# Reordering the value and gate products of a pair, and giving each step of the first block its own value tile

## Chip, cores, metric

One core of one Trainium2 chip. The metric is the device time of one execution in microseconds (us), as the median of several runs. PE is the matmul engine, DVE the vector engine, ACT the scalar engine, POOL the GpSimd engine, SP the engine that issues most DMAs.

## The reference, cut to what matters

```python
def reference(x, moe_w_gate, moe_w_val, moe_w_out):      # shortened
    X = np.fft.fft(x, axis=1)                            # x is 8 x 3008 x 256
    X = np.fft.fft(X, axis=2)
    y = X.real.reshape(24064, 256)
    gate = np.maximum(y @ w_gate, 0.0)                   # 256 x 1536
    val = y @ w_val
    return (gate * val) @ w_out                          # 1536 x 256
```

## The kernel before

The kernel folds the last transform into the two weights, and uses a symmetry of the real part: a column of the transform and its mirror image share an even part and differ in the sign of an odd part. So for one block of 512 columns and one slice of 128 features (a **step** `t`) it makes

- the gate: even product plus odd product gives the direct gate; a third product (`wm`, minus twice the odd weights) added to the same PSUM tile gives the mirrored gate;
- the value: even product `wc` into a PSUM tile `V`, then odd product `ws` on top. Between the two, DVE saves the even part: `E = nb * af + V`. Afterwards the mirrored value is `2E - V`.

There are 8 images x 3 blocks x 12 steps = 288 steps. From step 12 on they run as 144 - 6 = 138 **pairs** (pair `p` holds steps `2p` and `2p+1`), each with 16 projection matmuls (`out_piece`, line "po") of the block before. The first block (steps 0 to 11) has a simpler loop, without `E`, in which a third value product makes the mirrored value in place. The transform of the next image (`stage1`, `rotate`, `stage2`) is inserted at fixed steps by `between`, and POOL's folding of the images after that is dealt out by `pace`.

```python
psg = ...tile_pool(name="psg", bufs=2, space=PS)     # gate tiles
psv = ...tile_pool(name="psv", bufs=2, space=PS)     # value tiles, two banks each
...
ep = ...tile_pool(name="ep", bufs=3, space=SB)       # E and gm
...
def split(t):
    return t >= NF                                   # NF = 12

def pair(t, name):
    e = pairs.setdefault(t // 2, {})
    if name not in e:
        pool, shape, dt = {...,
                           "V": (psv, [128, 2, 512], F32), "gm": (ep, [128, 2, 512], F32),
                           "E": (ep, [128, 2, 512], F32)}[name]
        e[name] = pool.tile(shape, dt, tag=name.lower(), name=name)
    return e[name]

def gate(t):
    ...
    nc.tensor.matmul(G[:, ds], lhsT=wc[0][:, fs], rhs=pq[:, 0, ds], start=True, stop=False)
    nc.tensor.matmul(G[:, ds], lhsT=ws[0][:, fs], rhs=pq[:, 1, ds], start=False, stop=True)
    nc.scalar.activation(pair(t, "gs")[:, t % 2, ds], G[:, ds], ACTF.Relu)

def mirror_gate(t):                                  # must wait for the ReLU above
    ...
    nc.tensor.matmul(G[:, cols], lhsT=wm[0][...], rhs=pqt[b, blk][:, 1, cols], start=False, ...)
    nc.scalar.activation(pair(t, "gm")[:, t % 2, cols], G[:, cols], ACTF.Relu)

# value(t, k): the product with wc, ws or wm (k = 0, 1, 2) into pair(t, "V")[:, t % 2, :]
# even(t): E = nb * af + V           direct_h: h = gs * V         mirror_h: h = gm * (mirrored V)
# mirror_value(p): E = 2E - V on DVE for the whole pair, then mirror_h on POOL
...
def pace(t):
    paced["due"] += 0 if t < 22 else 1 if t < 46 else 0.85 if t < 100 else 0.7
    while paced["due"] >= 1:
        paced["due"] -= 1
        next(folds, None)
...
for t in range(NF + 1):                              # the first block
    if t:
        mirror_gate(t - 1)
    if t < NF:
        gate(t)
    if t:
        value(t - 1, 2)
        mirror_h(t - 1, 1, nc.vector, pair(t - 1, "V"))
    if t < NF:
        value(t, 0)
        value(t, 1)
        direct_h(t, 1)
        between(t)

for p in range(NF // 2, n + NF // 2):                # the pairs
    t = 2 * p
    live = p < n
    if NF // 2 < p <= n:
        mirror_gate(t - 1)
    if live:
        gate(t)
        value(t, 0)
    out_piece(t - NF, 0)                             # four projection matmuls
    between(t)
    if live:
        value(t + 1, 0)
    if NF // 2 < p <= n:
        direct_h(t - 2, 2)
    if live:
        even(t)
        even(t + 1)
    out_piece(t - NF, 1)
    if live:
        mirror_gate(t)
        gate(t + 1)
    out_piece(t + 1 - NF, 0)
    between(t + 1)
    if NF // 2 < p <= n:
        mirror_value(p - 1)
    if live:
        value(t, 1)
        value(t + 1, 1)
    out_piece(t + 1 - NF, 1)
```

## Time and profile before

| | before |
|---|---|
| median of 3 runs | 666.39 us (665.86 to 666.46) |
| profiled execution | 667.4 us |
| one steady pair without an insertion | 4.03 us (496 columns) to 4.11 us (512) |
| its matmuls back to back (512 columns: 10 x 0.216 + 16 x 0.109) | 3.90 us |
| first block, start of the first direct h to start of the last mirrored h | 32.1 us |

The head of the page: busy time of each engine, its share of the span, and its instructions.

```profile
PE 631.6 (95%) x4200; PEld 411.5 (62%) x4231; DVE 549.7 (82%) x642; ACT 433.2 (65%) x846; POOL 521.5 (78%) x436
```

PE at 95% looks full. The Trainium skill ("Perfetto Trace Analysis", Identifying the Most-Contended Engine) warns that matmul busy time is not a good measure of how close a kernel is to its limit, because matmuls are pipelined. This trace shows it: a 512-column matmul is listed with 0.38 us, but the next one starts 0.216 us later (and a 256-column one is followed after 0.109 us; medians over the trace). So PE must be judged by the **starts** of matmuls. Here is one pair of the last image, from the timeline (start, duration, engine, line and operation, output<-input, count; in brackets the idle time before, and what ended it). Only PE and DVE rows are kept.

```profile
605.80 0.38 PE L527 MATMUL V<-pq,wc 128*128 128x512 bf16 x1
606.02 0.60 PE L576 MATMUL po<-wo,h 128*128 128x256 bf16 x4
606.29 1.41 DVE L534 SCALAR_TENSOR_TENSOR E<-nb,af,V 128x512 f32<-128x512 bf16 x2 [0.48 <-PE V L527]
...
607.10 0.60 PE L576 MATMUL po<-wo,h 128*128 128x256 bf16 x4
607.61 1.21 DVE L554 SCALAR_TENSOR_TENSOR E<-E,V 128x1024 f32<-128x1024 f32 x1
607.75 0.59 PE L527 MATMUL V<-pq,ws 128*128 128x512 bf16 x2
```

The second even product starts at 605.80 and ends at 606.18. DVE has been idle for 0.48 us and starts the two `E` operations at 606.29; they end at 607.70. The odd product, which overwrites what `E` reads, starts at 607.75. PE's four projection matmuls before it, 0.109 us apart, end their slots at 607.54. The hole is 0.21 us, though the row of the odd product carries no bracket: in the modelled ends PE is still busy.

The first block has a hole of another kind. The lines are from step 5 of the first block:

```profile
52.70 0.67 DVE L547 TENSOR_TENSOR h<-gm,V 128x496 bf16<-128x496 f32 x1 [1.23 <-ACT gm L521]
53.43 0.37 PE L527 MATMUL V<-pq,wc 128*128 128x496 bf16 x1 [1.75 <-DVE h L547]
53.64 0.37 PE L527 MATMUL V<-pq,ws 128*128 128x496 bf16 x1
...
54.11 0.67 DVE L540 TENSOR_TENSOR h<-gs,V 128x496 bf16<-128x496 f32 x1 [0.74 <-PE V L527]
```

The even product of step 5 waits until DVE has finished the mirrored h of step 4, although the two use different halves of the `V` tile. DVE then waits 0.74 us for the product. The list of waits adds these up (total us, times, longest):

```profile
POOL h L547 <- DVE E L554: 107.7, 70, 4.1
DVE E L534 <- PE V L527: 61.5, 108, 2.6
PE V L527 <- DVE h L547: 7.7, 6, 1.7
PE psr L213 <- DMA t<-Td: 2.6, 1, 2.6
```

POOL's wait is spread unevenly. The windows view (length of the stretch, then busy us of each engine, with clock, DMA share and GB/s) shows that POOL is at 97 to 98% in one long stretch:

```profile
110.00:160.00 50.00, 48.41 (x342) 32.87 (x342) 42.03 (x48) 34.81 (x70) 49.06 (x46) 1.00 0.44 114
160.00:210.00 50.00, 49.70 (x350) 33.31 (x351) 43.34 (x49) 35.55 (x70) 48.58 (x43) 1.00 0.55 139
210.00:260.00 50.00, 49.49 (x337) 33.21 (x340) 43.46 (x49) 35.09 (x71) 49.07 (x44) 1.00 0.43 114
```

The fifth busy figure is POOL's: 49.06, 48.58 and 49.07 of 50 us.

Last, one stall at 400 us, where PE waits for the shuffled image, and after which the matmuls run at half speed (0.41 us apart) for a while:

```profile
399.74 0.60 PE L576 MATMUL po<-wo,h 128*128 128x256 bf16 x4
402.89 0.18 PE L213 MATMUL psr<-t,rot 128*128 128x12 bf16 x1 [2.56 <-DMA t<-Td]
...
403.97 0.62 PE L519 MATMUL G<-pq,wm 128*128 128x496 bf16 x1
404.38 0.62 PE L512 MATMUL G<-pq,wc 128*128 128x497 bf16 x1
```

### The profile page before, as it was taken

Reading aid. Unit: us, or ns where it says so; the run is one execution under the profiler, and the core shown is the slowest. Engines: PE = TensorE matmul, PEld = TensorE weight load, DVE = VectorE, ACT = ScalarE, POOL = GpSimd, SP = SyncE. Lnnn points to the kernel's source line nnn. Section 1 sums busy time; section 2 is a strip of 40 time slices with the busy share of each in tenths; the row PEclk is TensorE's granted clock in tenths of the full one; section 3 lists DMA queues with packets and bytes.
Section 4 is the critical chain, followed back from the end, with each engine's and each line's share of the span. In section 5 each row is a group of like instructions: output and inputs, shape, how many; then the busy total and the mean of one; then the engine's idle time right before and its main releaser. Section 6 shows DMA issues by size and latency. Waiting matters only on the chain.

```text
span 667.4 us, 11836 instructions
## 1 busy us (share of the span) xinstructions
PE 631.6 (95%) x4200; PEld 411.5 (62%) x4231; DVE 549.7 (82%) x642; ACT 433.2 (65%) x846; POOL 521.5 (78%) x436
## 2 busy tenths in 40 slices
PE   6867999999999999999999998999999999999995
PEld 3422576666666666666666665666666666666665
DVE  9845888888888888888888886888888888888881
ACT  5454586777677767676677765677677767656660
POOL 9559679999999999999988996988555555555552
PEclk9699999999999999999999998999999999999998
DMA  9593554542836184353724464211522142112114
GB/s 255 185 234 46 133 138 128 148 112 83 212 81 145 42 237 102 89 127 96 189 57 100 93 174 101 65 32 38 149 49 64 38 119 72 54 32 63 31 32 93
DMA packets 35635, 70.72 MB, mean 106 GB/s; under 512 B 6124, under 2 KB 23508, under 8 KB 32244
## 3 DMA queue, kind: packets, MB, share of 16 engines
q1 hardware_dynamic: 32152, 57.92, 33.2%
q0 software_dynamic: 3120, 11.80, 8.0%
q8 instruction: 33, 0.54, 0.3%
q10 hardware_dynamic: 304, 0.25, 0.2%
q14 instruction: 26, 0.21, 0.1%
HBM read 39.77 MB, written 30.96 MB: 106 GB/s over the span
## 4 chain that ended last, share of the span: by engine, by line
PE 78%; DVE 9%; POOL 5%; DMA 3%; issue 2%; ACT 2%; SPq 0%; DVEq 0%; POOLq 0%; ACTq 0%
PE po L576 32%; PE V L527 19%; PE G L513 8%; PE G L519 7%; PE G L512 7%; DVE E L534 6%; DMA t<-Td 2%; PE ps L183 2%; POOL eo L139 2%; PE ps L225 1%; POOL h L547 1%; PE psw L282 1%; DVE h L540 1%; DVE h L547 1%; DMA nb<-Nd 1%
## 5 line engine op out<-in xcount | busy, mean ns | idle before, releaser
L547 POOL TENSOR_TENSOR h<-gm,E 128x992 bf16<-128x992 f32 (+1 forms) x138 | 319.5, 2316 | 109.8 <-DVE E L554 107.7
L576 PE MATMUL po<-wo,h 128*128 128x256 bf16 (+2 forms) x2304 | 342.4, 273 | 0.7
L576 PEld LDWEIGHTS <-h 128*128 128x128 bf16 (+2 forms) x2304 | 233.2, 103 | 121.0 <-issue 0.5
L534 DVE SCALAR_TENSOR_TENSOR E<-nb,af,V 128x496 f32<-128x496 bf16 (+1 forms) x276 | 190.9, 733 | 79.2 <-PE V L527 61.5
L521 ACT ACTIVATE gm<-G 128x496 f32<-128x496 f32 (+1 forms) x288 | 170.2, 591 | 132.0 <-PE G L519 127.4
L540 DVE TENSOR_TENSOR h<-gs,V 128x1024 bf16<-128x1024 f32 (+3 forms) x150 | 172.7, 1151 | 8.6 <-PE V L527 7.5
L514 ACT ACTIVATE gs<-G 128x497 f32<-128x497 f32 (+2 forms) x288 | 169.6, 589 | 1.8 <-PE G L513 1.8
L554 DVE SCALAR_TENSOR_TENSOR E<-E,V 128x992 f32<-128x992 f32 (+1 forms) x138 | 164.3, 1190 | 0.0
L527 PE MATMUL V<-pq,wc 128*128 128x497 bf16 (+2 forms) x287 | 107.8, 376 | 7.7 <-DVE h L547 7.7
L513 PE MATMUL G<-pq,ws 128*128 128x497 bf16 (+2 forms) x287 | 107.8, 376 | 1.5 <-DVE pq L232 0.6
L519 PE MATMUL G<-pq,wm 128*128 128x496 bf16 (+1 forms) x288 | 108.2, 376 | 0.0
L512 PE MATMUL G<-pq,wc 128*128 128x496 bf16 (+2 forms) x271 | 101.7, 375 | 0.0
L527 PE MATMUL V<-pq,ws 128*128 128x496 bf16 (+2 forms) x276 | 82.6, 373 | 4.7 <-DVE E L534 2.2
L589 ACT COPY os<-po 128x512 f32<-128x512 f32 x63 | 36.9, 585 | 32.6 <-PE po L576 30.7
L513 PEld LDWEIGHTS <-ws 128*128 128x128 bf16 x288 | 28.2, 98 | 32.7 <-issue 0.3
L527 PEld LDWEIGHTS <-ws 128*128 128x128 bf16 x288 | 26.6, 97 | 32.6 <-issue 30.4
L193 ACT CAST t<-ps 96x512 bf16<-96x512 f32 x63 | 36.6, 581 | 12.3 <-PE ps L181 7.2
L527 PEld LDWEIGHTS <-wc 128*128 128x128 bf16 x288 | 28.2, 98 | 20.9 <-issue 3.2
L110 POOL TENSOR_TENSOR eo<-xla 94x254 bf16<-94x254 f32 x56 | 40.0, 724 | 1.0
L107 POOL TENSOR_TENSOR xla<-xla,xha 94x510 f32<-94x510 f32 x28 | 35.4, 1264 | 2.2
L110 POOL TENSOR_TENSOR eo<-xlb 94x254 bf16<-94x254 f32 (+1 forms) x42 | 33.6, 809 | 0.7
L519 PEld LDWEIGHTS <-wm 128*128 128x128 bf16 x288 | 28.2, 98 | 6.9 <-issue 4.1
(125 smaller groups left out, 381.8 us busy)
## 6 DMA issues: line engine op xcount, KB each, us to landing
out_dram<-os SPq DMA_DIRECT2D x126, 128.0 KB
out_dram<-os SPq DMA_DIRECT2D x86, 64.0 KB
Td<-t SPq DMA_DIRECT2D x7, 768.0 KB
t<-Td SPq DMA_DIRECT2D x7, 768.0 KB
xla<-in_x_dram SPq DMA_DIRECT2D x7, 720.0 KB
xlb<-in_x_dram SPq DMA_DIRECT2D x7, 640.0 KB
nb<-Nd SPq DMA_DIRECT2D x24, 128.0 KB
out_dram<-os SPq DMA_DIRECT2D x39, 48.0 KB
```

The source lines that it names most:

```text
L110: yield eng.tensor_tensor(e1[:, :, o:o + H - 1], x1[:, :, 1:H], free(x1, D - 1, [D, n], [-1, H - 1]), op=op)
L512: nc.tensor.matmul(G[:, ds], lhsT=wc[0][:, fs], rhs=pq[:, 0, ds], start=True, stop=False)
L513: nc.tensor.matmul(G[:, ds], lhsT=ws[0][:, fs], rhs=pq[:, 1, ds], start=False, stop=True)
L514: nc.scalar.activation(pair(t, "gs")[:, t % 2, ds], G[:, ds], ACTF.Relu)
L519: nc.tensor.matmul(G[:, cols], lhsT=wm[0][:, f * 128:(f + 1) * 128], rhs=pqt[b, blk][:, 1, cols], start=False, stop=True, skip_group_check ...
L521: nc.scalar.activation(pair(t, "gm")[:, t % 2, cols], G[:, cols], ACTF.Relu)
L527: nc.tensor.matmul(pair(t, "V")[:, t % 2, cs], lhsT=w[:, f * 128:(f + 1) * 128], rhs=pqt[b, blk][:, min(k, 1), cs], start=(k == 0), stop=( ...
L534: nc.vector.scalar_tensor_tensor(pair(t, "E")[:, t % 2, cols], nbt[b, blk][:, cols], af[:, f:f + 1], pair(t, "V")[:, t % 2, cols], op0=ALU ...
L540: nc.vector.tensor_tensor(pair(t, "h")[:, k, 0, 0:ds.stop - ds.start], pair(t, "gs")[:, k, ds], pair(t, "V")[:, k, ds], op=ALU.mult)
L547: eng.tensor_tensor(free(pair(t, "h")[:], 1024 * (t % 2) + 512 + w - 1, [1024, n], [-1, w]), pair(t, "gm")[:, k, cols], val[:, k, cols], o ...
L554: nc.vector.scalar_tensor_tensor(E[:, :, cols], E[:, :, cols], 2.0, V[:, :, cols], op0=ALU.mult, op1=ALU.subtract)
L576: nc.tensor.matmul(po[0:m, i, :], lhsT=pair(t - f + ff, "h")[:, ff % 2, sg, g * 128:g * 128 + m], rhs=wo[:, ff, :], start=(ff == 0), stop= ...
```

## The change

The intent: let DVE have both even products early, so that `E` is done before PE wants to add the odd products; and let the steps of the first block not wait for each other's `V` tile. No operation is added or removed.

```diff
     def pair(t, name):
 
         e = pairs.setdefault(t // 2, {})
+        if name == "V" and not split(t):
+            name = f"V{t % 2}"
+            if name not in e:
+                e[name] = psv.tile([128, 2, 512], F32, tag="v", name="V")
+            return e[name]
         if name not in e:
@@
             mirror_gate(t - 1)
         if live:
+            value(t, 0)
+            value(t + 1, 0)
             gate(t)
-            value(t, 0)
         out_piece(t - NF, 0)
         between(t)
-        if live:
-            value(t + 1, 0)
         if NF // 2 < p <= n:
             direct_h(t - 2, 2)
```

Below the inserted lines, line numbers of the changed kernel are 5 higher: L527 becomes L532, L534 L539, L554 L559, and so on.

## The prediction

> **What bounds the kernel now.** The page gives PE 95% busy, DVE 82%, POOL 78%, ACT 65% of 667.4 us. Busy PE overstates, so I read starts in the timeline. One 512-column matmul follows another by 0.213–0.216 us (the Trainium skill, "TensorE: Matmul & The Clock Gate", Part 1, has 215.7 ns; the trace agrees), a 256-column one by 0.108. A steady pair has 10 and 16 of these: 3.87 us. But pairs without inserted FFT work take 4.11 (E starts 606.29, 610.40, 614.52). The rest is a hole of 0.2 us ahead of the odd value product: PE stops at 607.53, V<-pq,ws starts at 607.75, right after the two E operations (606.29 + 1.41 = 607.70). These start 0.11 us after the second even product ended (605.80 + 0.38), DVE having idled 0.45 us. So the loop is second even product -> E, E -> odd product. I count 82 such holes, 16.5 us. Where stage1/stage2 is inserted in a pair's second half there is none.
>
> In the first block (38–71 us) the matmul starts show 15.7 us of gaps. The list of waits has V <- DVE h (L547) 7.7 us, 6 times, up to 1.75: every odd step's first value product waits for the mirrored h of the step before, which reads the other half of the same tile. DVE then idles 0.74 us before the direct h.
>
> **What the change does.** No work is added or removed.
>
> 1. First block: a tile per step removes the six waits. The gain per odd step is DVE's 0.74 us idle, not the wait; more where fold_w queued behind the blocked product (1.5 us at 53 us). Sum 5.5, less 0.8 because nb's DMA (5 us from pq to E at 118–123 us) then arrives just in time: **-4.7 us**.
> 2. Steady pairs: the second even product issues 0.43 us earlier, E about 0.4 earlier, ending before PE reaches the odd product. The hole closes: 0.197 each, 60 pairs outside stretch 4: **-11.8 us**.
> 3. Gate products issue 0.43 later; mirror_gate(t) follows only 8 matmuls after. gs starts 0.47 after the second gate product starts, takes 0.60, plus 0.05 to release PE: 1.12 against 1.08. New stall 0.035, some 78 pairs: **+2.7 us**.
> 4. POOL is 98% busy from 110 to 260 us (windows), mirrored h lagging E by 2–4 us with three E buffers. There POOL sets the pace; of 4.4 us of holes only about 1 is got: **-1 us**.
> 5. rotate waits for t<-Td at 400–403 us (2.6 us, then 3.4 us of half clock). DMA time doesn't shrink: **+0.6 us**.
>
> Sum -14.2: **652.3 us**, range 646.5 to 658.5, close to the 2% line (653.1): faster by over 2% 0.56, within 2% 0.43, slower by over 2% 0.01.
>
> **What would show each step.** (1) V<-pq,wc no longer waits for h L547; the first block ends 4–5 us earlier. (2) E pairs 3.9 us apart in the last block; no hole ahead of V<-pq,ws; E's wait for PE V (61.5 us) at most half. (3) G<-pq,wm in mid-pair starts 0.05 us after gs ends, with a PE gap of 0.02–0.06. (4) 110–260 us shrinks by 1–2 us only, POOL 99% busy, E or gm waiting more for POOL h. (5) psr's wait stays or grows.
>
> **What would make it wrong.** If os or t copies on ACT delay gs, the stall of (3) is 0.1 or more and eats half of (2). If POOL isn't the pace-maker, up to 3 us more. If rotate's wait and clock drop vanish, 4 us more; if more batches get one, 4 us less each. If ACT holds the first block, its gain halves.

## The result, and the profile after

| | before | after |
|---|---|---|
| median, same rounds, 4 runs each | 666.42 us | 648.12 us (646.91 to 649.26) |
| ratio | | 0.972 (95%: 0.9693 to 0.9747) |
| profiled execution | 667.4 us | 645.1 us |

Ratios are the mean time of one kernel's fast runs over that of the other's of the same rounds, so not quite the ratio of the medians. The change is faster by 18.3 us in the medians. The two profiles differ by 22.3 us: the profiled execution of before was a slow one of its kind (669.18 us as timed, against a highest of 668.38 among the timed runs), and the one of after the fastest of its four.

```profile
PE 618.7 (96%) x4231; PEld 410.4 (64%) x4231; DVE 549.3 (85%) x642; ACT 444.7 (69%) x846; POOL 521.9 (81%) x436
```

The steady pair, last image again:

```profile
584.66 0.59 PE L532 MATMUL V<-pq,wc 128*128 128x512 bf16 x2
...
585.31 0.38 PE L518 MATMUL G<-pq,ws 128*128 128x512 bf16 x1
585.41 1.40 DVE L539 SCALAR_TENSOR_TENSOR E<-nb,af,V 128x512 f32<-128x512 bf16 x2
585.52 1.04 PE L581 MATMUL po<-wo,h 128*128 128x256 bf16 x8
585.72 0.60 ACT L519 ACTIVATE gs<-G 128x512 f32<-128x512 f32 x1 [0.27 <-PE G L518]
586.40 0.38 PE L524 MATMUL G<-pq,wm 128*128 128x512 bf16 x1
...
587.04 0.60 PE L581 MATMUL po<-wo,h 128*128 128x256 bf16 x4
587.48 0.59 PE L532 MATMUL V<-pq,ws 128*128 128x512 bf16 x2
```

`E` now starts without waiting for PE and ends at 586.81; the odd product follows its predecessors at their own pitch (587.04 + 4 x 0.109 = 587.48, as listed). The hole is gone, and the five pairs of this image that took 4.11 us each now take 3.88 to 3.93. Counted by matmul starts over the whole traces from 72 us on, holes of more than 0.02 us ahead of the odd products fall from 79 (15.9 us) to 19 (4.8 us, 3.8 of them in four holes between 118 and 260 us). The mirrored gate product at 586.40 starts 0.08 us after `gs` ends (586.32), and 0.88 us after the first of eight projection matmuls, whose slots take 8 x 0.109 = 0.87: it comes just in time, and it does so everywhere: none of the mirrored gate products after 72 us has such a hole ahead of it.

Step 5 of the first block:

```profile
49.16 0.37 PE L532 MATMUL V<-pq,wc 128*128 128x496 bf16 x1
49.37 0.37 PE L532 MATMUL V<-pq,ws 128*128 128x496 bf16 x1
...
50.35 0.67 DVE L552 TENSOR_TENSOR h<-gm,V 128x496 bf16<-128x496 f32 x1 [1.23 <-ACT gm L526]
...
50.94 0.66 DVE L545 TENSOR_TENSOR h<-gs,V 128x496 bf16<-128x496 f32 x1
```

The products of step 5 run before the mirrored h of step 4, and DVE does the two h one after the other. The waits:

```profile
POOL h L552 <- DVE E L559: 51.7, 41, 2.1
DVE h L545 <- PE V L532: 40.5, 84, 1.9
DVE E L539 <- POOL h L552: 5.6, 10, 1.4
PE psr L213 <- DMA t<-Td: 1.4, 1, 1.4
```

"PE V <- DVE h of the mirror" is gone, and so is `E`'s wait for the even product (61.5 us before). DVE's slack hasn't vanished; it now lies before the direct h (40.5 us), where PE hardly waits for it (PE's own waits for the direct h come to 0.8 us). `E` waits longer for POOL (5.6 us, against 2.1 before). And POOL is as full as before in its stretch, which by the table below got no shorter:

```profile
110.00:160.00 50.00, 48.02 (x345) 32.95 (x343) 41.89 (x47) 36.69 (x71) 48.56 (x45) 1.00 0.45 117
160.00:210.00 50.00, 49.50 (x353) 33.38 (x352) 43.53 (x49) 36.17 (x70) 48.90 (x45) 1.00 0.57 144
210.00:260.00 50.00, 48.95 (x341) 32.75 (x341) 43.13 (x48) 36.14 (x69) 48.95 (x45) 1.00 0.49 134
```

A new stall lies in it, at the first block of the second image, where `E` needs the row `nb` that goes through DRAM:

```profile
116.09 0.39 PE L225 MATMUL ps<-m,t 128*128 128x128 bf16 x4
...
116.85 1.37 DVE L539 SCALAR_TENSOR_TENSOR E<-nb,af,V 128x496 f32<-128x496 bf16 x2 [2.71 <-DMA nb<-Nd]
...
118.28 0.58 PE L532 MATMUL V<-pq,ws 128*128 128x496 bf16 x2 [1.80 <-DVE E L539]
```

The rotation stall is shorter, and the clock stayed full after it:

```profile
390.35 0.18 PE L213 MATMUL psr<-t,rot 128*128 128x12 bf16 x1 [1.45 <-DMA t<-Td]
...
391.23 0.37 PE L524 MATMUL G<-pq,wm 128*128 128x496 bf16 x1
```

With the starts of `2E - V` (L554, L559), and of the first direct and the last mirrored h, as milestones, the 22.3 us of the two profiles split like this:

| stretch | before | after | difference |
|---|---|---|---|
| start to first direct h (unchanged code) | 39.0 | 38.5 | -0.5 |
| first block, to its last mirrored h | 32.1 | 26.0 | -6.1 |
| from there to pair 13 | 36.2 | 34.8 | -1.4 |
| pair 13 to 51 (POOL at 98%) | 159.7 | 159.9 | +0.2 |
| pair 51 to 83 | 133.2 | 128.8 | -4.4 |
| pair 83 to 85 (rotation stall) | 12.8 | 9.6 | -3.2 |
| pair 85 to 142 | 235.3 | 227.9 | -7.4 |
| to the end | 19.1 | 19.7 | +0.5 |

A warning about the milestone: in a steady pair `2E - V` starts 0.13 us before the odd product in the old order and 0.74 us before it in the new one. So some 0.6 us of the row up to pair 13 is no gain, and it comes back in the last row. At pair 51 `E` is late and the distance is 0.14 us in both, so by the odd product pairs 13 to 51 are 0.45 us shorter, not 0.2 longer, and pairs 51 to 83 gain about 3.8, not 4.4.

### The profile page after: what moved, and what is told of

It reads as the page before. It is cut to its first block, busy times and chain, and to the rows that moved or that the text cites. A ratio compares the mean times of both kernels' runs of the same rounds, so it can differ in the third digit from the quotient of the medians.

```text
span 645.1 us, 11866 instructions
## 1 busy us (share of the span) xinstructions
PE 618.7 (96%) x4231; PEld 410.4 (64%) x4231; DVE 549.3 (85%) x642; ACT 444.7 (69%) x846; POOL 521.9 (81%) x436
## 4 chain that ended last, share of the span: by engine, by line
PE 82%; DMA 5%; POOL 5%; DVE 3%; ACT 2%; issue 1%; SPq 1%; ACTq 0%; POOLq 0%; DVEq 0%
PE po L581 35%; PE V L532 17%; PE G L524 8%; PE G L518 8%; PE G L517 8%; DMA t<-Td 2%; DMA Td<-t 2%; PE ps L183 2%; POOL eo L139 2%; PE ps L225 1%; PE psw L282 1%; DVE E L539 1%; POOL h L552 1%; SPq L632 1%; DVE h L545 1%
## 5 line engine op out<-in xcount | busy, mean ns | idle before, releaser
L581 PE MATMUL po<-wo,h 128*128 128x256 bf16 (+2 forms) x2304 | 326.0, 272 | 0.0
L545 DVE TENSOR_TENSOR h<-gs,V 128x1024 bf16<-128x1024 f32 (+3 forms) x150 | 173.7, 1158 | 54.9 <-PE V L532 40.5
L539 DVE SCALAR_TENSOR_TENSOR E<-nb,af,V 128x496 f32<-128x496 bf16 (+1 forms) x276 | 190.2, 730 | 12.3 <-POOL h L552 5.6
L559 DVE SCALAR_TENSOR_TENSOR E<-E,V 128x992 f32<-128x992 f32 (+1 forms) x138 | 164.3, 1190 | 0.0
L517 PE MATMUL G<-pq,wc 128*128 128x497 bf16 (+2 forms) x288 | 107.9, 375 | 0.0
L532 PE MATMUL V<-pq,ws 128*128 128x497 bf16 (+2 forms) x288 | 85.4, 374 | 3.5 <-DVE E L539 3.4
L532 PE MATMUL V<-pq,wc 128*128 128x497 bf16 (+2 forms) x288 | 85.5, 375 | 0.0
L532 PEld LDWEIGHTS <-wc 128*128 128x128 bf16 x288 | 27.7, 98 | 22.5 <-issue 3.9
L517 PEld LDWEIGHTS <-wc 128*128 128x128 bf16 x288 | 28.2, 98 | 20.3 <-issue 2.9
L532 PEld LDWEIGHTS <-ws 128*128 128x128 bf16 x288 | 26.5, 97 | 9.7 <-issue 6.3
```

The costliest lines, as they stand in the source:

```text
L532: nc.tensor.matmul(pair(t, "V")[:, t % 2, cs], lhsT=w[:, f * 128:(f + 1) * 128], rhs=pqt[b, blk][:, min(k, 1), cs], start=(k == 0), stop=( ...
L539: nc.vector.scalar_tensor_tensor(pair(t, "E")[:, t % 2, cols], nbt[b, blk][:, cols], af[:, f:f + 1], pair(t, "V")[:, t % 2, cols], op0=ALU ...
L545: nc.vector.tensor_tensor(pair(t, "h")[:, k, 0, 0:ds.stop - ds.start], pair(t, "gs")[:, k, ds], pair(t, "V")[:, k, ds], op=ALU.mult)
L559: nc.vector.scalar_tensor_tensor(E[:, :, cols], E[:, :, cols], 2.0, V[:, :, cols], op0=ALU.mult, op1=ALU.subtract)
L581: nc.tensor.matmul(po[0:m, i, :], lhsT=pair(t - f + ff, "h")[:, ff % 2, sg, g * 128:g * 128 + m], rhs=wo[:, ff, :], start=(ff == 0), stop= ...
```

## The experiments

The theory after the result: (a) the first block's tiles and the pair's order are two independent gains that add; (b) in the pair, only the early second even product matters, the gate's place is free as long as `gs` ends in time; (c) from about 100 to 260 us POOL sets the pace and takes the gain there. Rivals are named with each run. "Same rounds" medians of before were 666.6 to 666.9 us.

### 1 and 2. Each part alone

Experiment 1 keeps only the hunk in `pair`, experiment 2 only the hunk in the loop over pairs.

```diff
# experiment 1, against before
+        if name == "V" and not split(t):
+            name = f"V{t % 2}"
+            ...
# experiment 2, against before
+            value(t, 0)
+            value(t + 1, 0)
             gate(t)
-            value(t, 0)
         ...
-        if live:
-            value(t + 1, 0)
```

Experiment 1, expected:

> Only the first block's value tile of its own per step; the old order of a pair. Theory (the two parts touch different stretches and add): the first block (first direct h to last mirrored h) shrinks from 32.1 to about 26.0 us as in the changed kernel, and the rest is as before: 660 us, 6 to 7 below the 666.4 of before; V<-pq,wc no longer waits for the mirrored h. Rival (what the first block gains is lost again, because POOL or the loads of nb set the pace later): 664 to 666 us. Rival (the tiles do little without the order): within 2 us of before.

Measured: 660.70 us, ratio 0.9904 (0.9881 to 0.9927), 5.9 below before. The first block took 26.03 us.

Experiment 2, expected:

> Only the new order of a pair; the first block keeps the shared tile. Theory: the first block stays at 32 us with its six waits; holes ahead of the odd value product are gone from the steady pairs, period 3.85 to 3.93 us in the last block; 655 us, 11 to 13 below before. Rival (the gain of the changed kernel is almost all the first block and the clock drop at 400 us that one profile of before happened to show): 661 us or more.

Measured: 654.13 us, ratio 0.9799 (0.9777 to 0.9821), 12.5 below before. The first block took 32.09 us, with its six waits (7.7 us).

What follows: 5.9 + 12.5 = 18.4 us, and the whole change gave 18.3. The parts add, and all of the gain is accounted for by the timed runs, so the 3 us of the rotation stall and the half clock in the two profiles need be no part of it: experiment 2 has its own drop of the clock (at 125 us, in its profile) and is as fast as the sum asks for. The granted clocks point the same way. In the rounds of these experiments before took 668.3 and 668.4 us in the two executions at a mean clock of 0.984, and 666.0 to 667.8 us in the five at 0.986 to 0.988; the profiled execution, at 0.984, is one of the former kind. Of the changed kernel's four, the two at 0.981 and 0.983 took 649.3 and 648.5 us, those at 0.986 and 0.987 took 647.8 and 646.9.

### 3. The gate products first again

```diff
         if live:
+            gate(t)
             value(t, 0)
             value(t + 1, 0)
-            gate(t)
         out_piece(t - NF, 0)
```

> The changed kernel with the gate products put back ahead of the two even value products, the latter still together and ahead of the projection. Theory (what counts is that the second even product comes before the first four projection matmuls; the gate's place costs and gives nothing, as gs ends just in time): the same as the changed kernel within 1.5 us, 647 to 649 us, with E starting about 0.4 us later in the cycle but still ending before the odd product. Rival, the term of the prediction (mirror_gate is held 0.035 us by gs in some 78 pairs): 2 to 3 us faster than the changed kernel, 645.5 us. Rival (E must start as early as it can): slower by 3 us or more, holes back.

Measured: 648.84 us (647.43 to 649.92), ratio 0.9716 (0.969 to 0.9743), against 0.972 for the change. The same, within noise. In its profile DVE waits 0.28 us for the second even product again (at 588.5 us), but `E` ends at 590.20 and the odd product starts at 590.48, at its own pitch. So the useful part of the reordering is that the second even product passes the four projection matmuls; that the gate goes behind both buys nothing and costs nothing. The prediction's stall of 2.7 us in the mirrored gate product isn't there: no execution of experiment 3, which keeps the gate out of its reach, was below 647.4 us.

### 4. POOL's load spread evenly

```diff
-        paced["due"] += 0 if t < 22 else 1 if t < 46 else 0.85 if t < 100 else 0.7
+        paced["due"] += 0 if t < 22 else 0.72
```

> The changed kernel with POOL's folds spread evenly (0.72 of a fold piece per step from step 22 on, in place of 1, then 0.85, then 0.7); the same work in all. Theory (POOL sets the pace from about 100 to 260 us: it is 98% busy there and E waits for it, so the new order gains nothing there): pairs 13 to 51 get shorter, the POOL lag stays under 1.5 us, the holes ahead of the odd product between 160 and 260 us (about 2 us) go, 3 to 4 us faster in all, 644.5 us; what is left is the wait for nb near 118 us. Rival (POOL is busy there but not the limit; stage1 and stage2 fill these pairs): within 1 us of the changed kernel.

Measured: 641.35 us (640.87 to 642.42), ratio 0.9614 (0.9591 to 0.9638), about 7 us below the changed kernel's 648.1: more than expected. (The two profiles differ by 5.5 us only; the changed kernel's is its fastest execution, and two of its four had a lower granted clock, as said above.) Pairs 13 to 51 took 154.8 us in place of 159.9, and pairs 18 to 51 (after the `nb` stall) 133.9 in place of 137.6. POOL's mirrored h followed `2E - V` by 0.6 us on average over pairs 13 to 51, in place of 2.8. In the windows POOL has slack again, and PE is listed as busy throughout:

```profile
160.00:210.00 50.00, 50.00 (x360) 34.32 (x359) 44.71 (x52) 37.10 (x71) 46.62 (x40) 1.00 0.46 123
210.00:260.00 50.00, 50.00 (x359) 34.11 (x358) 44.47 (x49) 37.24 (x73) 47.53 (x43) 1.00 0.52 129
```

By matmul starts, the holes ahead of the odd product from 72 us on sum to 0.9 us in place of 4.8; the three of 0.6 to 0.8 us at 201, 238 and 259 us are gone. The rest of the gain I read from the two profiles: pairs 16 to 18 took 9.2 us in place of 10.6, as the `nb` stall shrank, and pair 83 to 84 took 3.8 us in place of 5.5, without any wait at the rotation. Both are waits for DMAs that shared the queues with the image loads, and the image loads follow POOL's folds; that the moved loads are the cause is likely, but no run isolates it.

### 5. The even pace without the change

The same edit on the kernel before.

> The kernel before with POOL's folds spread evenly (0.72 of a fold piece per step), nothing of the change. Theory (with the old order a pair takes 4.0 to 4.1 us on PE and DVE, about what POOL needs, so relieving POOL gives little; the two gains need each other): 0 to 3 us below before, 663.5 to 666.5, pairs 18 to 51 within 1.5 us of the 138.4 us of before. Rival (the pace is a gain of its own, independent of the order): 7 us below before, 659.5, pairs 18 to 51 about 134 us.

Measured: 664.19 us, ratio 0.9963 (0.9946 to 0.9979), 2.7 below before; pairs 18 to 51 took 138.1 us against 138.4. The same edit is worth 7 us after the change and 2.7 before it, hardly any of the latter in POOL's stretch (0.8 us over pairs 13 to 51): in its profile there is no wait at the rotation, which is where its gain shows. My reading is that with the old order PE's own loop through `E` takes about as long as POOL's work. What is measured is that either edit alone shortens pairs 18 to 51 by less than 1 us (138.4 to 137.6 and to 138.1); both together shorten them by 4.5 us.

### 6. The gate products four projection matmuls later still

```diff
             value(t, 0)
             value(t + 1, 0)
-            gate(t)
         out_piece(t - NF, 0)
+        if live:
+            gate(t)
         between(t)
```

> The changed kernel with the gate products of a pair's first step put four projection matmuls later, so that only four (0.43 us) stand between them and the mirrored gate product that must wait for the direct gate's ReLU. From the trace of the changed kernel: gs starts 0.41 us after the second gate product starts, lasts 0.60, and 0.08 us later the mirrored product starts: 1.09 us, against 0.65 us of matmuls left in between. Theory: a new hole of 0.43 us ahead of the mirrored gate product in most pairs (0.22 less where a transform stage is inserted), about 50 us in all, 690 to 700 us, slower than before. Rival (ACT and PE overlap otherwise, the gate's place doesn't matter): within 5 us of the changed kernel.

Measured (one look): 693.09 us, 45 above the changed kernel. The timeline of a pair:

```profile
640.44 0.38 PE L518 MATMUL G<-pq,ws 128*128 128x512 bf16 x1
640.66 0.60 PE L581 MATMUL po<-wo,h 128*128 128x256 bf16 x4
640.86 0.60 ACT L519 ACTIVATE gs<-G 128x512 f32<-128x512 f32 x1 [0.70 <-PE G L518]
...
641.51 0.38 PE L524 MATMUL G<-pq,wm 128*128 128x512 bf16 x1 [0.25 <-ACT gs L519]
```

From the second gate product to the mirrored one it is 1.07 us here, with 0.65 us of matmuls in between: that is the length of the chain gate -> ReLU -> mirrored gate when PE waits for it. In the changed kernel 0.216 + 8 x 0.109 = 1.09 us of matmuls lie in between. The whole traces agree: where PE waits for `gs` in experiment 6, it starts 0.050 us after the end of `gs`; in the changed kernel none of the mirrored products after 72 us starts less than 0.071 us after it. So the change puts the gate at the last place where it is free: eight projection matmuls cover the ReLU, four leave a hole of 0.42 us.

### 7. `nb` asked for earlier, while POOL sets the pace

```diff
-    plan = {0: ((18, 19, 20, 21, 22, 23, 24, 25), 26, 32, (33, 34, 35, 37, 39, 41)),
+    plan = {0: ((16, 17, 18, 19, 20, 21, 22, 23), 24, 30, (31, 32, 33, 37, 39, 41)),
```

> The changed kernel with the second image's transform stages issued two steps earlier in the first image, so that nb of its first block is asked for two steps before it is needed; the uneven pace stays. In the changed kernel E waits 2.7 us for nb near 117 us. Theory (POOL, which is 98% busy from 100 to 260 us, sets the end of this stretch, so the wait only lets POOL catch up): the wait for nb is gone, but pair 51 comes at most 1 us sooner, 647.5 us. Rival (the wait is a plain loss on the critical path): 2 to 2.7 us faster, 645.7 us, and pair 51 comes that much sooner.

Measured: 648.02 us (647.32 to 648.35), ratio 0.9719 against 0.972 for the change: nothing. The wait for `nb` is gone, pair 18 comes 2.2 us sooner (119.4 in place of 121.6), and pair 51 comes 0.2 us sooner (258.9 in place of 259.2). What was gained is paid back in waits for POOL:

```profile
DVE E L539 <- POOL h L552: 9.1, 12, 2.3
```

That is 9.1 us in place of 5.6. This is the clearest evidence for (c): taking away a real stall in this stretch doesn't move its end.

### 8. A different order in the first block (a miss)

With a tile per step, the next step's value products and direct h could go ahead of the last value product and mirrored h of the step before. Based on experiment 4.

```diff
         if t:
+            if t < NF:
+                value(t, 0)
+                value(t, 1)
+                direct_h(t, 1)
             value(t - 1, 2)
             mirror_h(t - 1, 1, nc.vector, pair(t - 1, "V"))
         if t < NF:
-            value(t, 0)
-            value(t, 1)
-            direct_h(t, 1)
+            if not t:                # as above, for step 0
+                ...
             between(t)
```

> The evenly paced changed kernel with another order in the first block: the value products and the direct h of a step come before the last value product and the mirrored h of the step before, which the tile per step makes possible. In the changed kernel the first block's DVE idles 0.53 us per step for that last product. Theory (first block is a loop direct h -> last value product -> mirrored h -> next direct h of 1.78 us; the new order breaks it, steps then take about 1.4 us where no weight fold is in the way): first block 26.0 -> 22 to 24 us, 2 to 4 us faster in all, 638.5 us against 641.4. Rival (weight folds on ACT and DVE hold the first block): within 1 us.

Measured: 644.07 us, ratio 0.9658 (0.9642 to 0.9674): 2.7 us slower than experiment 4. The first block took 28.9 us.

```profile
42.72 0.66 DVE L552 TENSOR_TENSOR h<-gm,V 128x496 bf16<-128x496 f32 x1
43.44 0.37 PE L532 MATMUL V<-pq,wc 128*128 128x496 bf16 x1 [0.50 <-DVE h L552]
...
44.12 0.67 DVE L545 TENSOR_TENSOR h<-gs,V 128x496 bf16<-128x496 f32 x1 [0.74 <-PE V L532]
```

I had overlooked that there are only two `V` tiles. The products of step `t` need the tile of step `t - 2`, which is free after its mirrored h; the new order puts that after the direct h of step `t - 1`, so the wait on the tile returned, now at every step without a fold in the way, 2.0 us per step in place of 1.8. The steps with a fold lost as much or more (3.56 us in place of 3.16 for one of them); there the direct h waits for `gs`, and how much of that comes from the tile isn't shown. The mirrored h must come first as long as there are two tiles.

### 9 and 10. The evenly paced kernel again, and with `nb` earlier

Experiment 9 is experiment 4 once more, as the base on the same chip; experiment 10 adds the edit of experiment 7 to it.

> The evenly paced changed kernel again, on the chip of the next run and with more rounds, as its base: 641 to 642 us.

> The evenly paced changed kernel with nb asked for two steps earlier, the same edit that gave nothing while POOL set the pace. In the evenly paced kernel pair 17 still takes 5.7 us, some 1.5 more than its neighbours. Theory (with POOL relieved, a wait in this stretch is a plain loss): 1 to 1.5 us faster than its base, 640.2 us, pair 51 that much sooner, pair 17 at about 4.3 us. Rival (the wait is hidden by something else here too): within 0.5 us of the base.

Measured: 641.22 us (640.82 to 641.60; ratio 0.9615) and 640.82 us (640.35 to 641.12; ratio 0.9610). The profiles show pair 51 0.8 us sooner (254.1 in place of 254.9) and pair 17 at 3.85 in place of 5.9 us, but the intervals of the ratios overlap widely, so the 0.4 us of the times isn't settled. My size was off: of the 1.5 us that `E` waits for `nb`, PE lost only some 0.8 us as a hole in its matmul starts, because the odd product had slack. Experiment 10 is the fastest that was run, 25.9 us below before.

## Why the prediction was right, and where its sum was off

The predicted time, 652.3 us, is 4.2 us above the measured 648.1 and inside the range, 1.6 us from its lower end. The two mechanisms that carry the gain held; a third, the new stall, did not come, and two smaller terms were off. Errors of both signs met in the sum (a loss of 2.7 us and a gain of 1 us that both stayed away), so the total being this close speaks for the two large terms and not for each of the five.

1. **First block, predicted -4.7.** The six waits went, and DVE's gain was its idle time, as said. The size was 6.1 us in the profile and 5.9 alone (experiment 1). The 0.8 us that was subtracted because `nb` would arrive just in time wasn't lost there: `E` of pair 6 started right after the last mirrored h. The wait for `nb` came at the second image instead (2.7 us near 117 us), a place that the prediction had used as its example but hadn't charged.
2. **Holes of the steady pairs, predicted -11.8.** Right, a little small. In the profiles pairs 51 to 83 and 85 to 142 lost 4.4 and 7.4 us, and the 7 pairs up to 13 lost 1.4 with their entry: 13.2 us, or some 12.4 without the shifts of the milestone, with whatever the new stall of point 3 cost already taken off.
3. **New stall before the mirrored gate product, predicted +2.7.** This step failed. The prediction said "gs starts 0.47 after the second gate product starts, takes 0.60, plus 0.05 to release PE: 1.12 against 1.08". The 0.47 had been read at 604.94 to 605.41, where ACT was still in the mirrored ReLU before (604.92 to 605.52): a queueing time was taken for a latency. (After 420 us of that trace no 512-column `gs` found ACT idle, and the shortest distance is 0.48.) In the changed kernel `gs` starts 0.41 us after, and experiment 6, where PE does wait, measures the whole chain as 1.07 us against the 1.09 available. Experiment 3, without the risk, is no faster. This term alone, 2.7 us, is the largest part of the 4.2 us by which the prediction was too slow.
4. **POOL's stretch, predicted -1.** Right in kind, and even a bit too hopeful: +0.2 us from pair 13 to 51 (-0.45 by the odd product). Experiments 4, 5 and 7 show the cause. Emptying POOL gives 5 us here (1.4 of them in pairs 16 to 18, where the `nb` stall shrank), but only together with the new order; removing a stall gives nothing while POOL is full.
5. **Rotation, predicted +0.6.** In the profiles it was 3.2 us shorter, by a shorter wait and by the clock that stayed full. But the two parts measured alone sum to 18.4 us, against 18.3 for the whole change, without it, so in the timed runs it plays no part that can be seen. Whether a given execution drops its clock there varies; it isn't an effect of the change that these runs can show.

So the sum of what was measured alone is -5.9 for the first block and -12.5 for the order. The prediction had -4.7 and -9.5 (-11.8, +2.7, -1 and +0.6). The missing 3.0 us of the order are mostly the stall that didn't come (2.7); by the odd product the holes gave 0.6 us more and POOL's stretch about 0.6 less than predicted, which cancels. The missing 1.2 us of the first block are mostly the 0.8 us for an `nb` wait that came elsewhere.

## What to carry to other kernels

Look for holes in the starts of matmuls, not in busy time: here 0.2 us per pair, unseen in a PE that reads 95% busy, were the larger part of the gain. Before costing a dependent chain, read its latency where the receiving engine was idle, and count how many independent matmuls must lie in between (here eight cover the ReLU and four don't). When a gain fails to appear in one stretch, look for the engine with the second-highest load in that stretch alone; relieving POOL was worth about 7 us after this change, and only 2.7 before it.

## What the Trainium skill lacked or had wrong

- "TensorE: Matmul & The Clock Gate", Part 1 (What's actually happening) and "Why this matters for your kernels": the half clock is said to come after an idle window of about 3.4 us, with the advice to allow no gaps above about 3 us. Here PE waits of 2.56 us (before, at 400 us), 2.24 us (experiment 3) and 2.00 us (experiment 2) each went with a half clock for 3.4 us, as did one of 3.36 us (experiment 6), while waits of 2.09 us (experiment 7), 1.88 us (experiment 2, at the rotation), 1.80 and 1.45 us (the change) did not. The advice is too generous: from about 2 us on it can happen. That the outcome varies near 2 us fits the page's remark that the window is free-running. The packed traces' own record of the granted clock shows more: within a trace all changes lie on a grid of 3.413 us, and the four drops between 72 and 640 us came at the end of a grid slot that held 2.00 to 2.89 us of the wait. No other slot held more than 1.88 us of one; the 2.09 us of experiment 7 were cut by a slot's end into 0.92 and 1.17 us. These are four drops in the traces of one kernel, so the limit between 1.88 and 2.00 us is a reading and not a tested rule.
- The same page, Part 1, gives 215.7 ns between the starts of 512-column matmuls with a full clock; the trace agrees (0.216 us).
- I found no figure for the whole chain matmul -> ReLU on ACT -> dependent matmul. Here it takes 1.07 us from start to start at 512 columns (experiment 6): 0.42 until ACT starts, 0.60 for the ReLU, 0.05 until PE starts. With ACT idle 0.41 to 0.42, with ACT just finishing another operation 0.48.
- "Perfetto Trace Analysis" (Identifying the Most-Contended Engine) says that matmul busy time misleads, and gives as the reason that pipelined instructions look smaller in the trace. In this case they are listed longer than they take (0.38 us against 0.216 from start to start), so the busy share reads too full: in the last image, pairs of 4.11 us hold 3.90 us of matmuls, and yet the windows view lists PE as busy for 39.6 of 40 us (610 to 650 us).
